# A fused block-sparse attention and MLP kernel: mask factors padded to 128 rows, w_in loads moved on POOL's queue, and new times in the planner

## The chip, the cores and the metric

The kernel runs on one core of a Trainium2 chip. The time is that of the device in microseconds for one execution; lower is better. Six runs of the kernel before gave a median of 275.79 us (274.7 to 276.76). One further execution was taken by the hardware profiler; every profile line below is from it.

## The reference

Attention under a block mask, and behind it a two-layer MLP with a gated activation, all in float32 at the interface:

```python
# q, k, v: [4 batches, 8 heads, 768, 64]; blocks of 32, so 24 x 24 blocks
mask = np.abs(blk_i - blk_j) <= 1
mask = mask | (blk_i == 0) | (blk_j == 0) | (blk_i == 23) | (blk_j == 23)
# and, for every block row, three sampled block columns: mask = True
scores = np.where(mask, q @ k.T / sqrt(64), -1e9)
x = softmax(scores) @ v              # -> [3072 tokens, 512]
h = x @ w_in                         # w_in: 512 x 2048
g = h / (1 + exp(-beta * h))         # beta: one for each of 2048 columns
out = g @ w_out                      # w_out: 2048 x 512
```

## The kernel before, in words

**Work and units.** Products are in float16 with float32 sums in PSUM. The 16 pairs of heads (4 batches times 4 pairs, numbered 0 to 15) and the query columns make units of 256 or 512 queries. A unit has score steps (`products`, L694), each of which fills two PSUM banks; one exponential of 128x1024 on ScalarE (`exps`, L698) empties them. For batches 1 to 3 VectorE then multiplies by a 0/1 mask (`masks`, L708). Value products follow (`av`, L731), VectorE divides by the row sums (`divide`, L740 and L742), and the quotient is turned by TensorE (`turn_pe`, L754) or by a DMA (`turn_dma`, L762). Seven groups of 256 or 512 tokens take the MLP: 16 hidden steps of four products with w_in (L787), a tanh on ScalarE (L794), a gate on VectorE (L800), then the products with w_out (L811), their eviction and the store. The silu is computed as half of (1 + tanh(beta h / 2)) h, and the half is applied at the eviction.

**Two kinds of mask.** Batch 0 carries the mask inside the score product: 24 extra rows of keys and queries, so that K and Q have 88 rows (64 + 24). Batches 1 to 3 have score products of 64 rows, and the 0/1 mask `mask01` (128 x 6 x 768) is built once, by 12 products of TensorE (L653), six of 512 columns and six of 256, with contraction over the 24 blocks (`NB` rows of both factors):

```python
nc.tensor.matmul(ps[:, 0:n], lhsT=seen.rearrange("i j r -> i (j r)")[:, c:S:NC],
                 rhs=oh_q[:, q0 // P:(q0 + n) // P, :], start=True, stop=True)
```

`oh_q` is copied by POOL (L885) from a one-hot table, `seen` is written by VectorE (`seen_step`, L647). Each product is evicted to `mask01` by VectorE (L512).

**Order.** TensorE's order is a string written out by hand (`order`, L956 on): S is a score step, V a value step, T a turn, H a hidden step, O or o a step of the output products, X an extra. The extras come from a list in fixed order (L938 to L954): turns of the keys and first queries of pairs 1 to 3, the turn of beta, turns of the late queries (columns 256 to 767) of pairs 0 to 3, mask products, turns of pair 4, mask products. Each has a time `at` before which the planner does not place it.

`weave` (L67) is a planner that runs when the program is built. It walks through the string with a model of the engines' clocks (costs such as .903 for an exponential, .432 for a score step of batch 0; start time `t0`; arrival times `W_IN`, `W_OUT` and the extras' `at`). It never alters TensorE's order. It decides two things: the order of the instructions on ScalarE and VectorE, and which PSUM bank each step takes. `Banks.one` (L48) takes the bank that is free first in the plan's time; among those that count as free it prefers the one whose partner in the pair came (or comes) free last:

```python
with_it = now + 20.0 if e[b ^ 1] is None else min(e[b ^ 1], now + 20.0)
able.append((max(e[b], now), -with_it, b))
```

`Banks.pair` (L42) does the same for the two banks of a score step. On the chip an instruction waits until the earlier readers of its bank have ended, whatever the plan thought.

**POOL's queue** (L860 to L890) is a list too, and its instructions run in that order: casts of keys, values and late queries to float16, and between them the issues of DMA loads. The four quarters of w_in (`load_w_in`, 512 KB each) are issued at L876, L878, L881 and L884; the one-hot copy and the loads of pair 4 and of w_out follow. Hidden step f reads quarter f // 4 of w_in. The loads that SP issues at the start (k, q, v of pairs 0 to 3) are L563 to L576.

Of the kernel before, what the change touches and what calls it, by code (L numbers as in the profile page):

```python
# [11 lines left out]
FP16 = mybir.dt.float16  # L12
AF = mybir.ActivationFunctionType
# [50 lines left out]
            self.ends[b] = t  # L64


def weave(order, units, moes, extras, beside, flush, t0=6.5):  # L67

    PE_OUT, ACT_OUT, DVE_OUT = .20, .16, .12
    W_IN = (21.0, 24.3, 27.7, 31.0)
    W_OUT = (37.0, 40.3, 43.7, 47.0)
    clock = {"PE": t0, "ACT": t0, "DVE": t0 + 1.0}
    queue = {"ACT": [], "DVE": []}
    banks = Banks()
# [28 lines left out]
    def one_bank(*after):  # L107

        if None in after:
            return None  # L110
        t = max(after)
        b = banks.one(max(t, clock["PE"]))
        return b and (max(t, b[0]), b[1])
# [149 lines left out]
    def hidden():  # L263
        g, f = hs[0]
        if groups_left[g]:
            return None
        b = one_bank(arrived[g], W_IN[f // 4] if g == 0 else 0.0, gb.free() if f == 0 else 0.0)
        return b and (b[0], lambda t: do_hidden(g, f, b[1], t))

    def do_hidden(g, f, b, t):  # L270
        hs.pop(0)
        m = moes[g]
        if f == 0:
            g_use[g] = gb.take()
        banks.take(b)
        m["h"](f, b)
        end = whole(t, 4 * (m["n"] / 2400.0 + .002))
        if f == 15:
            xt.end(xt_use[g], end)

        def tanh_done(e):
            kt = tsb.take()
            put("DVE", lambda: e + ACT_OUT, .07 + m["n"] * .00104, 1, lambda: m["gate"](f),
                lambda e2: gate_done(e2, kt))

        def gate_done(e, kt):
            tsb.end(kt, e + DVE_OUT)
            banks.end(e + DVE_OUT, b)
            gates[g] = gates.get(g, 0) + 1
            if gates[g] == 16:  # L290
                g_ready[g] = e + DVE_OUT
        put("ACT", lambda: None if tsb.free() is None else max(end, tsb.free()),
            .143 + .00083 * m["n"], 0, lambda: m["tanh"](f), tanh_done)

    def outs(rows=False):
        g, ts, part = os_[0]
        if g not in g_ready:
            return None
        after = max(g_ready[g], W_OUT[part] if g == 0 else 0.0)
        if part:  # L300
# [36 lines left out]
    while True:  # L337
# [3 lines left out]
        if state["next"] < len(order):  # L341
            c = kinds[order[state["next"]]]()
# [31 lines left out]
def kernel(  # L374
# [11 lines left out]
    nc = tc.nc  # L386

    B, H, S, D = q.shape
    BLK = 32
    NB = S // BLK  # L390
    P = 128
    NC = S // P
    NPAIR = H // 2
# [11 lines left out]
    persist = ctx.enter_context(tc.tile_pool(name="persist", bufs=1))  # L405
# [50 lines left out]
    def load(i, name, c0=0, c1=NC, split=False, eng=nc.sync, and_then=None):  # L456
        b, j = seq[i]
        x = {"k": k, "q": q, "v": v}[name]
        if (i, name) in first_in_w_out:
            at = 1024 + 2 * 2 * NC * D * first_in_w_out.index((i, name))  # L460
            loaded[(i, name)] = (w_out_sb.rearrange("p f m -> p (f m)")
                                 [:, at:at + 2 * 2 * NC * D].bitcast(FP32)
                                 .rearrange("p (h x) -> p h x", h=2))
        elif (i, name) not in loaded:
            loaded[(i, name)] = stage_pool.tile(
                [P, 2, NC * D], FP32, tag="sq" if name == "q" else "skv", name=f"{name}st")
        st = loaded[(i, name)]
        src = x[b, 2 * j:2 * j + 2].rearrange("h (p c) d -> p h (c d)", c=NC)
        for h in ((0, 1), (1, 2)) if split else ((0, 2),):
            eng.dma_start(out=st[:, h[0]:h[1], c0 * D:c1 * D],  # L470
                              in_=src[:, h[0]:h[1], c0 * D:c1 * D])
            if and_then is not None:
                and_then()
                and_then = None

    def cast(i, name, eng, c0=0, c1=NC, h0=0, h1=2):
        dst = (va_tiles[i % NVA] if name == "v" else
               (k_rows if name == "k" else q_rows)[i % NST] if i < NPAIR else
               packed(i)[name == "q"].rearrange("p c (h d) -> p h c d", h=2))
        st = loaded[(i, name)].rearrange("p h (c d) -> p h c d", d=D)  # L480
        eng.tensor_copy(out=dst[:, h0:h1, c0:c1, 0:D], in_=st[:, h0:h1, c0:c1, :])  # L481

    def packed(i):

        return [r[i % NST].rearrange("p h c s -> p (h c s)")[:, 0:NC * P]
                .rearrange("p (c s) -> p c s", s=P) for r in (k_rows, q_rows)]
# [39 lines left out]
    def turned_by_pe(i, which, h, c0, c1):  # L526

        rows = (k_rows, q_rows)[which][i % NST]

        def pe(b):  # L530
            tp = bank16(b)[:, 0:NC, :]
            for c in range(c0, c1):
                nc.tensor.transpose(out=tp[0:KR, c, :], in_=rows[:, h, c, 0:KR],  # L533
                                    identity=identity)
            return tp

        def copy(tp, on_act, a=c0, z=c1):
            evacuate(kq[i][which][0:KR, h, a * P:z * P],
                     tp[0:KR, a:z, :].rearrange("p c s -> p (c s)"), on_act)
        return pe, copy  # L540
# [11 lines left out]
    def load_w_in(i):  # L552
        nc.gpsimd.dma_start(out=w_in_sb[:, :, i * 512:(i + 1) * 512],
                            in_=w_in_r[:, :, i * 512:(i + 1) * 512])
# [23 lines left out]
    zeros = persist.tile([P, 256], FP16, name="zeros")  # L578
# [29 lines left out]
    oh_c = onehot.rearrange("i j r -> i (j r)").rearrange("i (p c) -> i c p", c=NC)  # L608
# [9 lines left out]
    for val in (0.0, float(NB - 1)):  # L618
# [3 lines left out]
            out=far, in0=iota_i[:, 0:1].to_broadcast([NB, NB]), scalar=val,  # L622
# [8 lines left out]
    mask16 = persist.tile([NB, NB], FP16, name="mask16")  # L631
# [8 lines left out]


    mask01 = persist.tile([P, NC, S], FP16, name="mask01")
    oh_q = persist.tile([NB, NC, P], FP16, name="oh_q")
    seen = persist.tile([NB, NB, BLK], FP16, name="seen")

    def seen_step():
        nc.vector.tensor_scalar(out=seen, in0=mask16.unsqueeze(2).to_broadcast([NB, NB, BLK]),  # L647
                                scalar1=0.0, scalar2=None, op0=ALU.is_equal)

    def mask01_task(c, q0, n):  # L650
# [12 lines left out]
    def beta_task():  # L663
        def pe(b):
            ps = psum[:, b, :]
            nc.tensor.transpose(out=ps[:, 0:N_FFC], in_=beta_sb, identity=ident[0:16, 0:16])
            return ps

        def copy(ps, on_act):
            nc.vector.tensor_scalar(out=beta_h_sb, in0=ps[:, 0:N_FFC], scalar1=0.5,  # L670
                                    scalar2=None, op0=ALU.mult)
        return pe, copy
# [169 lines left out]
    units = []  # L842
# [32 lines left out]
    cast(2, "v", nc.gpsimd)  # L875
    load_w_in(0)  # L876
    cast(3, "v", nc.gpsimd)
    load_w_in(1)  # L878
    for i in range(2):
        cast(i, "q", nc.gpsimd, 2, NC)  # L880
    load_w_in(2)  # L881
    for i in range(2, NPAIR):
        cast(i, "q", nc.gpsimd, 2, NC)
    load_w_in(3)  # L884
    nc.gpsimd.tensor_copy(out=oh_q, in_=oh_c)  # L885
    load(4, "k", eng=nc.gpsimd)
    load(4, "q", eng=nc.gpsimd)
    for i in range(4):
# [40 lines left out]
    extras = []  # L929

    def extra(first, need, at, took, task, eng, dur):
        box = {}
        extras.append(dict(
            first=first, need=need, at=at, took=took,
            pe=lambda b: box.update(ps=task[0](b)),
            out=(eng, dur, lambda: task[1](box["ps"], eng == "ACT"))))

    for i in range(1, NPAIR):  # L938
        at = (6.3, 9.2, 12.6)[i - 1]
        for h in range(2):  # L940
            extra(3 * i - 2, 3 * i, at, .34, turned_by_pe(i, 0, h, 0, NC), "DVE", .55)
        for h in range(2):
            extra(3 * i - 2, 3 * i, at, .12, turned_by_pe(i, 1, h, 0, 2), "DVE", .28)
    extra(8, 14, 9.0, .07, beta_task(), "DVE", .18)
    for i in range(NPAIR):
        for h in range(2):
            extra(6, 12 + 6 * i, (17.9, 18.5, 19.5, 21.3)[i], .23,
                  turned_by_pe(i, 1, h, 2, NC), "DVE", .42)
    for c in range(NC):
        extra(18, 36, 20.0, .22, mask01_task(c, 0, 512), "DVE", .6)  # L950
# [2 lines left out]
    for c in range(NC):  # L953
        extra(31, 60, 40.0, .11, mask01_task(c, 512, 256), "DVE", .35)  # L954
    cast(1, "q", nc.vector, 0, 2)
    order = (  # L956
        "SXXSXXSSXXXSXSVSXXSXSXVSXSXXXTSXXSSTVSSXSXVXSSSXVSVTSSTVSXHXHSSXHXHHSVSSVTSSSHXVHTSH"
        "HSHSXVTSHXHXVHSSHTHHHHSSHHHSSHHHHHHHSSXXVXSHSSVXHSoSoSSHVSSooSSVHSSXVVSoSSoSoSoSoSVV"
        "SSoSooSSVVOSSoSHHHHSSooSoSoSSoSoSVHVHHHVSSOHSSVHVSSHOSSVOSSSHOHVHHVHHSSHHHHSSOOSSSOH"
        "VSSHVSSHOHHHVSSooSSoSSoVHHHVVHHSSoooSoSoSoSoSSoooSSoSoSHHVSSHVHHHVHVSSooSoSoSoSoSSoS"  # L960
        "oSOVHHVHOVHVHHHHHSooSSooSSooSSooSoooSSoSooSHOVHOHHHHVHHTHHTVHHHHTVOHTOHHHHHHOHOOHOOH"
        "OHOHOHOHOOHOHHOOHOOOOOOOOOO"
    )
# [29 lines left out]
```

## Time and profile before

| | |
|---|---|
| median of six runs | 275.79 us |
| the profiled execution | 275.45 us |
| its span, first to last instruction | 273.7 us |
| TensorE busy | 266.3 us (97%) |
| VectorE busy | 204.6 us (75%) |
| ScalarE busy | 210.8 us (77%) |
| POOL busy | 61.0 us (22%) |
| chain that ended last | PE 86%, ACT 7%, DVE 2%, DMA 2%, issue 2% |

How to read what follows. PE is TensorE's products, PEld its weight loads, DVE VectorE, ACT ScalarE, POOL GpSimd, SP the engine that issues most DMAs. The chain follows the work back from the last instruction, at each step to what released it. L numbers are lines of the kernel before. A group such as "24*128 24x512 f16" is a product with weights of 24 rows and 128 columns and a moving operand of 24 rows and 512 columns; "88*128" and "64*128" are the score products of batch 0 and of the others. Brackets such as [1.32 <-ACT et L698] give the idle time ahead of an instruction and what ended it. Ends of TensorE's products are modelled, so records of neighbours overlap; the chain counts each stretch once. Between 13.6 and 19.7 us POOL issues the four loads of w_in with casts between them; they landed 6.7 to 9.2 us after their issue. Key and query columns reach TensorE first at 3.91 us, the exponentials begin at 7.49 us, the first hidden step is at 31.33 us and the first output product at 70.17 us.

### The profile page before, as it was taken

How to read it: one execution, taken by the hardware profiler on the slowest of the kernel's cores; microseconds unless marked ns; L12 is line 12 of the kernel's file. 1: busy time of each engine (PE TensorE's matmuls, PEld its weight loads, DVE VectorE, ACT ScalarE, POOL GpSimd, SP SyncE). 2: the span in 40 equal slices, each digit the busy share in tenths (PEclk: the TensorE clock that was granted, in tenths of full speed). 3: DMA queues.
4: the chain of work that ended last, by engine and by line, in shares of the span. 5: the costliest groups of instructions: out<-in, count | busy, mean ns of one | idle time of the engine just before them, and what ended most of it. 6: DMA issues, size and time to landing. Idle time of an engine off the chain costs nothing.

```text
span 273.7 us, 6832 instructions
## 1 busy us (share of the span) xinstructions
PE 266.3 (97%) x2774; PEld 150.4 (55%) x2774; DVE 204.6 (75%) x411; ACT 210.8 (77%) x276; POOL 61.0 (22%) x90
## 2 busy tenths in 40 slices
PE   8989999999999999999999999999999999999994
PEld 5876568544556645555345454464555555565541
DVE  6756657899999988899899786787867677863521
ACT  3879999898999799898898968979848866552300
POOL 4998508674022200330421000000000000000000
PEclk9999999999999999999999999999999999999999
DMA  6999998995499915375993131111120110011111
GB/s 199 367 245 214 250 263 294 244 273 180 86 245 230 187 51 185 95 194 109 230 248 89 29 79 42 58 42 25 73 41 38 41 77 2 0 41 40 51 65 77
DMA packets 46451, 36.23 MB, mean 132 GB/s; under 512 B 27844, under 2 KB 42388, under 8 KB 46420
## 3 DMA queue, kind: packets, MB, share of 16 engines
q1 hardware_dynamic: 40816, 26.89, 37.4%
q0 software_dynamic: 5568, 8.91, 14.8%
q8 instruction: 21, 0.34, 0.5%
q14 instruction: 10, 0.08, 0.1%
q10 hardware_dynamic: 36, 0.00, 0.0%
HBM read 27.27 MB, written 6.29 MB: 123 GB/s over the span
## 4 chain that ended last, share of the span: by engine, by line
PE 86%; ACT 7%; DVE 2%; issue 2%; DMA 2%; SPq 0%; POOL 0%; ACTq 0%
PE banks L811 29%; PE banks L787 27%; PE banks L731 13%; PE banks L694 13%; ACT et L698 5%; DMA kst<-in_k_dram 2%; ACT t_sb L794 2%; PE banks L533 1%; PE banks L653 1%; DVE et L708 1%; DVE g L800 1%; PE banks L754 1%; DVE xst L742 0%; SPq L470 0%; POOL kr L481 0%
## 5 line engine op out<-in xcount | busy, mean ns | idle before, releaser
L698 ACT ACTIVATE et<-banks 128x1024 f16<-128x1024 f32 x144 | 139.4, 1029 | 8.1 <-PE banks L694 7.2
L794 ACT ACTIVATE t_sb<-banks,beta_h_sb 128x512 f16<-128x512 f32 (+1 forms) x112 | 68.4, 634 | 36.4 <-PE banks L787 34.7
L787 PE MATMUL banks<-xt,w_in_sb 128*128 128x512 f16 (+1 forms) x448 | 93.5, 349 | 0.4 <-DVE g L800 0.4
L811 PE MATMUL banks<-w_out_sb,g 64*128 64x512 f16 (+1 forms) x612 | 93.7, 377 | 0.0
L708 DVE TENSOR_TENSOR et<-et,mask 128x1024 f16<-128x1024 f16 x108 | 77.4, 728 | 17.2 <-ACT et L698 15.6
L800 DVE SCALAR_TENSOR_TENSOR g<-t_sb,banks 128x512 f16<-128x512 f16 (+1 forms) x112 | 65.8, 605 | 20.4 <-ACT t_sb L794 20.0
L787 PEld LDWEIGHTS <-w_in_sb 128*128 128x128 f16 x448 | 40.8, 98 | 41.5 <-issue 6.7
L811 PEld LDWEIGHTS <-g 64*128 64x128 f16 (+1 forms) x612 | 37.0, 95 | 38.0 <-issue 1.3
L694 PE MATMUL banks<-qT,kT 64*128 64x256 f16 (+3 forms) x384 | 54.7, 325 | 0.3 <-DVE xst L742 0.2
L731 PEld LDWEIGHTS <-et 128*128 128x128 f16 x1152 | 40.9, 97 | 9.2 <-issue 2.7
L731 PE MATMUL banks<-va,et 128*128 128x65 f16 x1152 | 43.7, 193 | 0.1
L694 PEld LDWEIGHTS <-kT 64*128 64x128 f16 (+1 forms) x384 | 20.8, 95 | 19.4 <-issue 7.9
L481 POOL CAST kr<-kst 128x768 f16<-128x768 f32 (+1 forms) x15 | 13.3, 887 | 56.9 <-DMA kst<-in_k_dram 56.9
L742 DVE TENSOR_TENSOR xst<-banks,recip 128x256 f16<-128x256 f32 x48 | 20.4, 424 | 1.9 <-DVE recip L740 0.3
L481 POOL CAST va<-vst 128x768 f16<-128x768 f32 x13 | 12.3, 953 | 18.9 <-DMA vst<-in_v_dram 11.6
L740 DVE RECIPROCAL recip<-banks 128x4 f32<-128x4 f32 x48 | 8.5, 178 | 7.3 <-PE banks L731 7.0
L481 POOL CAST qr<-qst 128x768 f16<-128x768 f32 (+1 forms) x16 | 13.1, 830 | 2.3 <-DMA qst<-in_q_dram 2.0
L830 DVE SCALAR_TENSOR_TENSOR osb<-banks,osb 128x512 f32<-128x512 f32 x15 | 10.3, 685 | 1.5 <-ACT osb L824 1.4
L834 DVE TENSOR_SCALAR osb<-banks 128x512 f32<-128x512 f32 x9 | 6.2, 687 | 6.0 <-PE banks L811 6.0
L824 ACT ACTIVATE osb<-banks 128x512 f32<-128x512 f32 x15 | 9.1, 604 | 2.0 <-PE banks L811 2.0
L512 DVE CAST mask<-banks 128x512 f16<-128x512 f32 (+1 forms) x12 | 6.6, 554 | 3.2 <-PE banks L653 2.9
L512 DVE COPY qT<-banks 88x512 f16<-88x512 f16 (+2 forms) x16 | 5.4, 363 | 3.6 <-PE banks L533 3.2
(63 smaller groups left out, 78.7 us busy)
## 6 DMA issues: line engine op xcount, KB each, us to landing
out_dram<-osb SPq DMA_DIRECT2D x24, 256.0 KB, 2.0
kst<-in_k_dram SPq DMA_DIRECT2D x10, 384.0 KB, 3.7
vst<-in_v_dram SPq DMA_DIRECT2D x9, 384.0 KB, 4.9
qst<-in_q_dram SPq DMA_DIRECT2D x8, 384.0 KB, 4.0
w_in_sb<-in_moe_w_in_dram POOLq DMA_DIRECT2D x4, 512.0 KB, 8.1
w_out_sb<-in_moe_w_out_dram POOLq DMA_DIRECT2D x4, 512.0 KB, 13.6
kst<-in_k_dram POOLq DMA_DIRECT2D x4, 384.0 KB, 7.5
qst<-in_q_dram POOLq DMA_DIRECT2D x4, 384.0 KB, 8.4
```

The lines of the kernel that those rows point to most:

```text
L481: eng.tensor_copy(out=dst[:, h0:h1, c0:c1, 0:D], in_=st[:, h0:h1, c0:c1, :])
L512: nc.vector.tensor_copy(out=o, in_=i_)
L694: nc.tensor.matmul(sc[:, y, :], lhsT=lhsT, rhs=rhs, start=True, stop=True)
L698: nc.scalar.activation(out=et, in_=scs[x], func=AF.Exp, bias=0.0, scale=SCALE)
L708: nc.vector.tensor_tensor(out=et, in0=et, in1=m.unsqueeze(1).to_broadcast([P, 2, w, n]), op=ALU.mult)
L731: nc.tensor.matmul(at[:, z, qc, :], lhsT=ets[(hh, kc)][:, qc * P:(qc + 1) * P], rhs=va[:, hh, kc, 0:D + 1], start=(kc == 0), stop=(kc == N ...
L742: nc.vector.tensor_tensor(out=o, in0=at[:, :, :, 0:D], in1=recip.unsqueeze(3).to_broadcast([P, nh, nq, D]), op=ALU.mult)
L787: nc.tensor.matmul(hp[:, 0:n], lhsT=w_in_sb[:, c, f * P:(f + 1) * P], rhs=xt_tiles[group][:, c, 0:n], start=(c == 0), stop=(c == NPAIR - 1))
L794: nc.scalar.activation(out=t_sb[:, 0:n], in_=box[f][0][:, 0:n], func=AF.Tanh, bias=0.0, scale=beta_h_sb[:, f:f + 1])
L800: nc.vector.scalar_tensor_tensor(out=box["g"][:, f, 0:n], in0=t_sb[:, 0:n], scalar=1.0, in1=hp[:, 0:n], op0=ALU.add, op1=ALU.mult)
L811: nc.tensor.matmul(psum[:, b, :], lhsT=box["g"][r, f, ts * P:(ts + 1) * P], rhs=w_out_sb[r, f, :], start=z >= begun, stop=f == N_FFC - 1 o ...
L830: nc.vector.scalar_tensor_tensor(out=o_sb, in0=psum[:, bs[0], :], scalar=0.5, in1=o_sb, op0=ALU.mult, op1=ALU.add)
```

## The change

Three edits. First, `oh_q` and `seen` get 128 rows; two ScalarE copies of a zero tile clear them, and the one-hot copy and `seen_step` then write the first 24 rows as before. The mask products read the whole tiles, so they contract over 128 rows, 104 of them zero. Second, on POOL's queue the loads of w_in quarters 1, 2 and 3 stand behind the late-query casts of pairs 1, 2 and 3; before, quarter 1 stood ahead of these casts, quarter 2 behind the second cast and quarter 3 behind the fourth. Third, constants of the planner: `t0`, `W_IN`, `W_OUT`, and the `at` of the early turns, of beta and of the late-query turns. The order string and all costs in it stay.

```diff
--- before.py
+++ after.py
@@ -64,15 +64,15 @@
             self.ends[b] = t
-def weave(order, units, moes, extras, beside, flush, t0=6.5):
+def weave(order, units, moes, extras, beside, flush, t0=6.7):
     PE_OUT, ACT_OUT, DVE_OUT = .20, .16, .12
-    W_IN = (21.0, 24.3, 27.7, 31.0)
-    W_OUT = (37.0, 40.3, 43.7, 47.0)
+    W_IN = (22.0, 25.0, 27.5, 30.0)
+    W_OUT = (37.0, 39.5, 42.0, 44.5)
     clock = {"PE": t0, "ACT": t0, "DVE": t0 + 1.0}
     queue = {"ACT": [], "DVE": []}
     banks = Banks()
@@ -640,11 +640,15 @@
     mask01 = persist.tile([P, NC, S], FP16, name="mask01")
-    oh_q = persist.tile([NB, NC, P], FP16, name="oh_q")
-    seen = persist.tile([NB, NB, BLK], FP16, name="seen")
+
+    oh_q = persist.tile([P, NC, P], FP16, name="oh_q")
+    seen = persist.tile([P, NB, BLK], FP16, name="seen")
+    for x in (oh_q, seen.rearrange("p j r -> p (j r)").rearrange("p (c s) -> p c s", s=P)):
+        nc.scalar.activation(out=x, in_=zeros[:, 0:P].unsqueeze(1).to_broadcast([P, NC, P]),
+                             func=AF.Copy, bias=0.0, scale=1.0)
     def seen_step():
-        nc.vector.tensor_scalar(out=seen, in0=mask16.unsqueeze(2).to_broadcast([NB, NB, BLK]),
+        nc.vector.tensor_scalar(out=seen[0:NB], in0=mask16.unsqueeze(2).to_broadcast([NB, NB, BLK]),
                                 scalar1=0.0, scalar2=None, op0=ALU.is_equal)
     def mask01_task(c, q0, n):
@@ -875,14 +879,11 @@
     cast(2, "v", nc.gpsimd)
     load_w_in(0)
     cast(3, "v", nc.gpsimd)
-    load_w_in(1)
-    for i in range(2):
+    for i in range(NPAIR):
         cast(i, "q", nc.gpsimd, 2, NC)
-    load_w_in(2)
-    for i in range(2, NPAIR):
-        cast(i, "q", nc.gpsimd, 2, NC)
-    load_w_in(3)
-    nc.gpsimd.tensor_copy(out=oh_q, in_=oh_c)
+        if i:
+            load_w_in(i)
+    nc.gpsimd.tensor_copy(out=oh_q[0:NB], in_=oh_c)
     load(4, "k", eng=nc.gpsimd)
     load(4, "q", eng=nc.gpsimd)
     for i in range(4):
@@ -936,15 +937,15 @@
             out=(eng, dur, lambda: task[1](box["ps"], eng == "ACT"))))
     for i in range(1, NPAIR):
-        at = (6.3, 9.2, 12.6)[i - 1]
+        at = (8.0, 10.5, 12.8)[i - 1]
         for h in range(2):
             extra(3 * i - 2, 3 * i, at, .34, turned_by_pe(i, 0, h, 0, NC), "DVE", .55)
         for h in range(2):
             extra(3 * i - 2, 3 * i, at, .12, turned_by_pe(i, 1, h, 0, 2), "DVE", .28)
-    extra(8, 14, 9.0, .07, beta_task(), "DVE", .18)
+    extra(8, 14, 10.5, .07, beta_task(), "DVE", .18)
     for i in range(NPAIR):
         for h in range(2):
-            extra(6, 12 + 6 * i, (17.9, 18.5, 19.5, 21.3)[i], .23,
+            extra(6, 12 + 6 * i, (16.4, 17.0, 18.2, 19.5)[i], .23,
                   turned_by_pe(i, 1, h, 2, NC), "DVE", .42)
     for c in range(NC):
         extra(18, 36, 20.0, .22, mask01_task(c, 0, 512), "DVE", .6)
```

## The prediction

> **What bounds the kernel now.** I read the page's chain first (PE 86%, ACT 7%), then the chain in order of time around each place that the diff touches, then what PE, ACT and POOL waited for there. From 18.65 us to the end TensorE hardly ever has nothing to do, so the question is which of its time is not product time, and whether ScalarE lets a shorter TensorE be shorter. The chain at the first 0/1 mask products (L653; columns: start, length, piece):
>
> ```profile
> 26.36 0.35 PE banks L653
> 26.71 0.86 PE banks L731 x24
> 27.57 0.43 PE banks L694 x2
> 28.01 0.76 PE banks L731 x24
> ...
> 31.05 0.34 PE banks L653
> 31.39 0.54 PE banks L787 x4
> 31.94 0.35 PE banks L653
> 32.28 0.54 PE banks L787 x4
> ```
>
> One 512-column mask product takes 0.35 us of the chain; two 512-column score products take 0.43, so one such is worth 0.22. And what follows it is late as well: 24 value products take 0.86 after a mask product and 0.76 after the 88-row scores; four 256-column products take 0.54 instead of 0.44. The instruction forms say what differs (nanoseconds, least/median/most):
>
> ```profile
> L653 PEld LDWEIGHTS <-seen x12: 119/120/142, 26.3 to 79.3; 24*128 24x128 f16 x12
> L653 PE MATMUL banks<-oh_q,seen x12: 268/360/415, 26.3 to 79.3; 24*128 24x512 f16 x6, 24*128 24x256 f16 x6
> ```
>
> These are 24-row weights between 128-row and 88-row ones. The 88-row scores pass into 128-row work at no price (28.01), the 24-row ones pay going in and coming out. Second place, the only real stall of TensorE after the start, first from PE, then from ACT:
>
> ```profile
> 16.72 0.61 PE L694 MATMUL banks<-qT,kT 88*128 88x256 f16 x4
> 18.65 0.83 PE L533 MATMUL banks<-identity,qr 128*88 128x128 f16 x12 [1.32 <-ACT et L698]
> 19.32 0.27 PE L754 MATMUL banks<-identity,xst 128*128 128x128 f16 x2
> 19.43 0.60 PE L694 MATMUL banks<-qT,kT 88*128 88x256 f16 x4
> ```
>
> ```profile
> 15.71 2.88 ACT L698 ACTIVATE et<-banks 128x1024 f16<-128x1024 f32 x3
> 20.07 1.02 ACT L698 ACTIVATE et<-banks 128x1024 f16<-128x1024 f32 x1 [1.47 <-PE banks L694]
> ```
>
> The late-query transposes wait 1.32 us for the exponential that ends at 18.6, the last one queued; so ScalarE, until then the bound, empties and idles 1.47. Third, how much room ScalarE has (busy us of PE, PEld, DVE, ACT, POOL in each stretch):
>
> ```profile
> 19.00:31.00 12.00, 12.00 (x187) 8.47 (x184) 7.71 (x24) 10.89 (x12) 8.43 (x12) 1.00 1.17 231
> 31.00:50.00 19.00, 19.00 (x231) 12.85 (x230) 13.38 (x34) 17.44 (x27) 10.36 (x14) 1.00 1.11 261
> 50.00:62.00 12.00, 11.78 (x66) 5.38 (x65) 10.87 (x19) 12.00 (x19) 7.83 (x9) 1.00 1.10 266
> 62.00:80.00 18.00, 17.77 (x200) 8.88 (x200) 17.23 (x35) 17.14 (x23) 4.75 (x6) 1.00 0.56 170
> ```
>
> ScalarE has 1.56 us of idle time in 31 to 50, none in 50 to 62, 0.86 in 62 to 80. PE's clock column is 1.00 throughout.
>
> **Part 1, padding.** A mask product pays 0.13 on entry (0.35 less 0.22; for 256 columns 0.24 less 0.11), its follower 0.11. Seven (six of 512 columns and the first of 256, 26.3 to 48.1) stand between work of 88 or 128 rows: both charges go, 7 x 0.24 = 1.68. The other five stand among the 64-row scores: the pair at 64.59 and the one at 79.34 come from 64 rows, which still is a change, and save the exit (0.11 each); the one at 65.80 saves its entry (0.12); the one at 68.8 both (0.24). Sum 1.68 + 0.58 = 2.26 us of PE. The other end is nothing. The Trainium skill, "TensorE: Matmul & The Clock Gate", LDWEIGHTS: a weight load of 32 rows takes as long as one of 128, since columns set it. By that rule padding is worth 0; by the row the 24-row load takes 120 ns against 98 and[...] lies open. A second rule speaks against: "TensorEngine Tiling", Performance Considerations, wants up to 32 contraction rows as four row tiles side by side, which padding gives up. But in the trace the neighbouring pair takes 0.35 = 0.24 + 0.11, one after the other, and the others stand alone. I lose nothing and keep 2.26.
>
> Its price: two ACT copies, 128x768. ACT's 256-column rows take 0.47 to 0.49, the 1024-column ones 1.02, so by the line between some 0.84 each, 1.7 for both, and below 2.04. They are queued behind the warm-up (ends 2.90), need only the zeros of 0.87, and end by 4.6 (at most 4.94); behind them the key copy waits for PE until 4.81. Nothing, at most 0.13, and even that meets ACT's later idle 0.95 and 0.42 ahead of the first exponential. The DVE and POOL steps still write 24 rows: no change.
>
> **Part 2, w_in.** On POOL, a load's issue takes 0.74 (first 0.89), a late query cast 0.56 to 0.62. Casts 0, 1, 2 move up by 0.74 if their rows have landed; cast 3 keeps its place. Load 1 is issued at about 16.4 instead of 15.28, load 2 about 0.5 later, load 3 and the one-hot copy as before. Landing took 6.7 to 9.2 us, so load 1 is there by 25.6; its first reader is the fifth hidden step at 35.3. Cover 9.7 us. Behind it on POOL two loads of the next pairs wait for w_in (0.51 and 1.95), so they may go up to 0.6 later; POOL then waits 8.53 for a value load till 41.95, whose first product is at 64.94, and the pair-4 casts at 32 are first transposed at 45.0. No SP instruction is moved. I count 0; without the cover it would be those 1.1 us.
>
> **Part 3, the planner's times.** TensorE's order is a fixed string; the times only decide banks and the order on ACT and DVE. Worked through with the code's own costs (they only pick banks; no time is taken from them): with 17.9, the last exponential before the transposes is planned to free its pair at 17.78, so it counts as free, and `one` prefers the bank whose partner came free last, exactly that pair. The chip ends it at 18.61: the stall. With 16.4 the transposes come right behind the scores, planned at 17.3, when that exponential has not ended; the free banks are those of the first quotient, of beta and of an exponential two steps back. On the chip these are free by 17.0 and the casts done by 17.2. So the 12 transposes start near 17.35, the two of L754 and the scores follow (18.65 to 20.03 took 1.38), ending near 18.75: the next exponential starts about 18.75, not 20.07: gain 1.3. Against it: at 8.0 instead of 6.3 the first key transposes are planned after the first exponential, so the second score step takes that exponential's pair rather than a fresh one. It ends at 8.51, the scores started at 8.30: 0.25 late at once, and ScalarE runs almost unbroken from there. Net 1.05, bounds 0.7 to 1.4. The W_IN and W_OUT times lie before the planned start of what they gate (first hidden step about 30; L811 is 20 us behind W_OUT), so they move nothing.
>
> **Sum.** Part 3 moves PE and ACT together: 1.05. Of the 1.68 up to 50 us ScalarE must follow: it has 1.56 idle up to there, of which waits of the hidden steps keep some; I take 1.1. The ACT-bound stretch 50 to 62 starts that much earlier and keeps its length. Of the 0.58 later, ScalarE's 0.86 lets 0.45 through. That is 2.6. From 62 on the chain is PE up to 132, and ACT had just idled (0.93, waiting for PE) before its stretch there, so the shift carries to the end. Profiled execution: 275.45, of which span 273.7 and 1.75 around it. Span 271.1, execution 272.85; the median of the runs is 0.34 above the profiled one: **273.2**.
>
> **Rivals.** (a) ScalarE gives the padding back: 18.65 to 62 is ACT's work, so only part 3 and a few tenths come through, 1.3 in all: 274.5. For: ACT is 12.00 of 12 in 50 to 62. Against: its idle 1.05 at 48.7, just ahead, waited for PE. 0.15. (b) The padding doesn't do what it is for (the charge belongs to the changing tile, not to the rows): part 3 alone, 274.7. Against: the changes between 88-row and 128-row tiles are free. 0.05. (c) More than I count: all 2.26 plus 1.3, and smaller waits in 50 to 62 go with the nearer plan: 271.9. 0.12. (d) Slower: the new bank choice puts a stall like the one at 17.3 elsewhere. The plan runs ahead of the chip (first hidden step planned about 30, executed 31.33), so `one` can again hand out banks of exponentials not ended. Each costs up to ACT's 1.47 where ACT is the bound (7 to 19, 50 to 62, 132 to 142). The gain of 2.6 is used up by two such; with three the sum is 1.8 slower: 277.6. For: every bank after 8 us is chosen anew. Against: today's choice, no better informed, has one in 273 us. 0.10. The forecast has the remaining 0.58, with one or no small new wait, 272.2 to 274.4 by itself.
>
> A difference of 0.5% (1.4 us: 274.4 and 277.2) is about what a measurement of this kernel can tell. Faster: forecast 0.57, (c) 0.12, a little of (a) 0.04: 0.73. Slower 0.09. Same 0.18. The range 271.8 to 275.0 leaves out most of (d) and the best of (c).
>
> **What will show it.** L653 on 128 rows, 0.22 and 0.11 in the chain and 0.76 or 0.44 behind it: part 1. No PE wait at 17.3 and exponentials unbroken to 30: part 3; a second exponential at 9.2 instead of 8.94: its cost. Hidden steps never waiting for w_in: part 2. ACT's idle at 48.7 nearly gone: the room used. I am wrong if ACT idles as much before 50 while PE waits there, or if new PE waits for banks appear.

## The result, and the profile after

The changed kernel took 274.15 us (median of 37 runs, 272.26 to 276.35), the kernel before 276.10 in the same comparison. The ratio is 0.9928, with a 95% interval of 0.9913 to 0.9944: 2.0 us faster (1.5 to 2.4) where 2.6 was forecast. The profiled execution took 273.73, its span is 271.9 (before: 275.45 and 273.7).

First the chain at the first mask products (columns: start, length, piece). The line that builds them is now L657; L698 are scores, L735 values, L791 hidden products.

```profile
26.57 0.22 PE banks L657
26.79 0.75 PE banks L735 x24
27.54 0.43 PE banks L698 x2
27.98 0.76 PE banks L735 x24
...
31.02 0.22 PE banks L657
31.24 0.44 PE banks L791 x4
31.67 0.22 PE banks L657
31.89 0.44 PE banks L791 x4
```

A mask product of 0.35 us has become one of 0.22; the values behind it take 0.75 as against 0.86, the hidden products 0.44 as against 0.54. Both charges are gone, to the hundredth. Next comes TensorE where it had waited 1.32 us, and then ScalarE there:

```profile
18.40 0.61 PE L698 MATMUL banks<-qT,kT 88*128 88x256 f16 x4
18.85 0.83 PE L533 MATMUL banks<-identity,qr 128*88 128x128 f16 x12
...
19.63 0.60 PE L698 MATMUL banks<-qT,kT 88*128 88x256 f16 x4
```

```profile
10.34 1.02 ACT L702 ACTIVATE et<-banks 128x1024 f16<-128x1024 f32 x1 [1.76 <-PE banks L698]
11.54 11.61 ACT L702 ACTIVATE et<-banks 128x1024 f16<-128x1024 f32 x12 [0.18 <-PE banks L698]
```

There is no wait behind the scores now, and the exponentials run unbroken through 18.6 and past 20. But the second exponential starts at 10.34, not at 8.94 as in the profile of before: this execution lost 1.4 us in its start and so shows less than was won. A start as late is in the second profile of the kernel before too (below). Two of the stretches (busy us of PE, PEld, DVE, ACT, POOL, then clock, DMA share, GB/s):

```profile
31.00:50.00 19.00, 19.00 (x244) 14.15 (x242) 14.07 (x36) 18.23 (x29) 10.05 (x14) 1.00 1.18 263
...
62.00:80.00 18.00, 17.91 (x234) 9.81 (x233) 17.58 (x35) 17.77 (x22) 6.73 (x8) 1.00 0.75 218
```

ScalarE's idle time between 31 and 50 us has shrunk from 1.56 to 0.77: the room was used.

The order of the instructions on TensorE, ScalarE (but for the two copies of zeros) and VectorE is the same in both kernels. Worked through with its own rules, the planner's new times change the banks of TensorE's first 36 steps, up to about 21 us; behind those they only swap the names of the pairs (0, 1) and (2, 3), but for ten steps near the end.

**A measure that every run has.** VectorE takes 48 reciprocals, one for each value step, in one order in all kernels. Their times, less those of the first profile of before (in brackets), say where each execution stands: a minus is earlier. A kernel's own gain is read from one column to the next; the first column is its start.

| run | 1st (13.2) | 3rd (22.3) | 12th (49.4) | 22nd (95.3) | 23rd (108.8) | last (239.0) |
|---|---|---|---|---|---|---|
| before, again | +1.39 | +1.39 | +1.39 | +1.18 | +1.18 | +1.26 |
| w_in order alone | +0.31 | +0.31 | +0.31 | -0.16 | -0.15 | -0.18 |
| 64 rows alone | -0.43 | -0.43 | -0.42 | -1.03 | -1.02 | -1.00 |
| 128 rows alone | +0.77 | +0.76 | -0.67 | -0.73 | -0.72 | -0.96 |
| planner's times alone | +1.26 | -0.23 | -0.22 | +0.53 | +0.54 | +0.55 |
| late-query times alone | -0.25 | -1.40 | -1.33 | -1.22 | +0.24 | +0.23 |
| 128 rows, w_in, late-query times | +0.83 | -0.60 | -1.96 | -2.01 | -0.91 | -0.79 |
| the change | +1.69 | +0.20 | -1.22 | -1.60 | -1.60 | -1.72 |
| the change, again | +1.30 | -0.18 | -1.62 | -1.97 | -0.26 | -0.20 |
| change with zero products | -0.02 | -1.50 | -2.93 | -3.68 | -1.94 | -2.04 |
| change, pair 11 later | +1.26 | -0.22 | -1.66 | -1.13 | -1.13 | -0.97 |
| 128 rows, w_in, late-query times, pair 11 later | -0.06 | -1.50 | -2.85 | -1.78 | -1.78 | -1.88 |
| change with both | +0.67 | -0.82 | -2.25 | -1.11 | -1.11 | -1.25 |

### The profile page after: what moved, and what is told of

The parts are those of the page before. It is cut to its first block, busy times and chain, and to the rows that moved or that the text cites. A ratio compares the mean times of both kernels' runs of the same rounds, so it can differ in the third digit from the quotient of the medians.

```text
span 271.9 us, 6832 instructions
## 1 busy us (share of the span) xinstructions
PE 265.2 (98%) x2774; PEld 152.5 (56%) x2774; DVE 204.5 (75%) x411; ACT 211.7 (78%) x278; POOL 61.4 (23%) x90
## 4 chain that ended last, share of the span: by engine, by line
PE 87%; DVE 4%; ACT 3%; DMA 2%; issue 1%; SPq 0%; POOL 0%; ACTq 0%
PE banks L815 30%; PE banks L791 26%; PE banks L698 14%; PE banks L735 13%; DVE et L712 2%; DMA kst<-in_k_dram 2%; ACT et L702 2%; PE banks L533 2%; ACT t_sb L798 1%; PE banks L657 1%; PE banks L758 1%; DVE g L804 1%; DVE xst L746 0%; SPq L470 0%; DVE mask L512 0%
## 5 line engine op out<-in xcount | busy, mean ns | idle before, releaser
L815 PE MATMUL banks<-w_out_sb,g 64*128 64x512 f16 (+1 forms) x612 | 94.7, 377 | 0.1
L791 PE MATMUL banks<-xt,w_in_sb 128*128 128x512 f16 (+1 forms) x448 | 93.4, 349 | 0.4 <-DVE g L804 0.4
L791 PEld LDWEIGHTS <-w_in_sb 128*128 128x128 f16 x448 | 41.2, 98 | 41.1 <-issue 5.7
L815 PEld LDWEIGHTS <-g 64*128 64x128 f16 (+1 forms) x612 | 37.9, 95 | 38.5 <-issue 2.1
L698 PE MATMUL banks<-qT,kT 64*128 64x256 f16 (+3 forms) x384 | 56.8, 328 | 0.1
L735 PEld LDWEIGHTS <-et 128*128 128x128 f16 x1152 | 41.3, 97 | 8.6 <-issue 2.2
L735 PE MATMUL banks<-va,et 128*128 128x65 f16 x1152 | 43.6, 193 | 0.1
L698 PEld LDWEIGHTS <-kT 64*128 64x128 f16 (+1 forms) x384 | 22.0, 96 | 18.8 <-issue 7.7
L481 POOL CAST kr<-kst 128x768 f16<-128x768 f32 (+1 forms) x15 | 12.7, 849 | 55.1 <-DMA kst<-in_k_dram 55.1
L481 POOL CAST va<-vst 128x768 f16<-128x768 f32 x13 | 11.6, 898 | 18.9 <-DMA vst<-in_v_dram 10.8
L481 POOL CAST qr<-qst 128x768 f16<-128x768 f32 (+1 forms) x16 | 14.5, 908 | 2.8 <-DMA qst<-in_q_dram 2.8
```

The costliest lines, as they stand in the source:

```text
L698: nc.tensor.matmul(sc[:, y, :], lhsT=lhsT, rhs=rhs, start=True, stop=True)
L735: nc.tensor.matmul(at[:, z, qc, :], lhsT=ets[(hh, kc)][:, qc * P:(qc + 1) * P], rhs=va[:, hh, kc, 0:D + 1], start=(kc == 0), stop=(kc == N ...
L791: nc.tensor.matmul(hp[:, 0:n], lhsT=w_in_sb[:, c, f * P:(f + 1) * P], rhs=xt_tiles[group][:, c, 0:n], start=(c == 0), stop=(c == NPAIR - 1))
L815: nc.tensor.matmul(psum[:, b, :], lhsT=box["g"][r, f, ts * P:(ts + 1) * P], rhs=w_out_sb[r, f, :], start=z >= begun, stop=f == N_FFC - 1 o ...
```

## The experiments

**The padding alone.** As in the diff of the change, without its other two parts.

> The kernel before with the padding alone (two ScalarE copies of zeros, factors of 128 rows). Theory A (the prediction's): both tile changes go at seven mask products and one or two at the others; the mask products take 0.22 and 0.11 in the chain, TensorE is 1.5 to 1.7 us earlier at 50 us, 1.1 to 1.6 of it reach the end: 274.5 to 275.0 against 276.1, with the wait of 1.32 at 17.3 still there. Theory B (the planner's times alone are what helped, since ScalarE is full from 20 to 62): a gain of 0.3 or less.

The result is 0.9967 of before (0.9937 to 0.9997), 274.83 us. The wait of 1.32 is still there, the mask products take 0.22. In the table it wins 1.43 us between 22 and 49. So theory A holds and theory B falls, by the profile: the time alone (0.1 to 1.7 us won) would not exclude B's 0.3.

**The planner's times alone.** All constants of the change, 24-row factors, old order on POOL.

> The kernel before with the planner's times alone. Worked through with the planner's own rules, they change banks in the first 36 steps of TensorE only (to about 21 us), and behind that swap the names of two pairs, with no change of order on any engine. Theory A: the wait at 17.3 goes, ScalarE's idle 1.47 at 18.6 with it, the second exponential is 0.25 later: 1.05 faster (0.7 to 1.4). Theory B (the early choice costs what the late one gives: in the profile of the change the late query turns start at 18.85, 0.2 later than before): within 0.3 of before.

The result is 0.9967 (0.9938 to 0.9996), 275.42 us. The wait is gone: 1.49 us are won between the first and the third column. Then 0.75 is lost between 49 and 95, part of it in a wait of 0.9 us of the hidden products for a gate. The step is theory A's, and the whole lies inside A's bounds, but its interval reaches from 0.1 to 1.7 us.

**The late-query times alone.**

```diff
-            extra(6, 12 + 6 * i, (17.9, 18.5, 19.5, 21.3)[i], .23,
+            extra(6, 12 + 6 * i, (16.4, 17.0, 18.2, 19.5)[i], .23,
```

> The kernel before with only the four times of the late query turns changed (17.9, 18.5, 19.5, 21.3 to 16.4, 17.0, 18.2, 19.5). The first 26 steps keep their banks, so the second score step keeps a fresh pair. Theory A: the wait of 1.32 goes with no price at the start: 1.3 faster, 0.25 more than all planner times together, second exponential at 8.9. Theory C (the wait at 17.3 only absorbed time that ScalarE then makes up, since it has 1.56 us of idle between 31 and 50): 0.3 or less.

The result is 0.9989 (0.9966 to 1.0013), 275.77 us: not told from before. Yet 1.15 is won by 22 us. Theory C's number came, but not at its place: the lead is there at 49 and at 95 us (-1.33 and -1.22) and is lost at one point behind, where TensorE waits 1.33 us for a quotient that a DMA transposes.

**The change with the early times set back.**

```diff
-def weave(order, units, moes, extras, beside, flush, t0=6.7):
+def weave(order, units, moes, extras, beside, flush, t0=6.5):
...
-        at = (8.0, 10.5, 12.8)[i - 1]
+        at = (6.3, 9.2, 12.6)[i - 1]
...
-    extra(8, 14, 10.5, .07, beta_task(), "DVE", .18)
+    extra(8, 14, 9.0, .07, beta_task(), "DVE", .18)
```

(`W_IN` and `W_OUT` are set back too.)

> The change with the early planner times (6.3, 9.2, 12.6, beta, start, w_in, w_out) set back as before: padding, the order of the w_in loads and the late query times stay. Theory A: 0.25 faster than the change, which measured 0.9928 of before: 0.9919 or so, 273.9. If the early bank choice costs more, since TensorE then waits longer there and its clock falls (in the profile of the change it was 0.5 from 8 to 11 us), up to 1.4 faster than the change: 272.8. If it costs nothing, the same as the change.

The result is 0.9929 (0.9904 to 0.9954), 273.92 us: the same as the change, so the early bank choice has no price that a time shows. The wait for the transposed quotient is here as well, 0.97 us.

**The order of pair 11's transpositions on SP.** On the kernel of the last experiment:

```diff
-            if cast_at[i] + 2 == x and i > NPAIR:
+            if cast_at[i] + (4 if i == 11 else 2) == x and i > NPAIR:
```

> Padding, w_in order and late-query times as in the run of those three, and one DMA order changed: SP turns the keys and queries of pair 11 two score steps later, so that the last quotient transposition of the first 512-column hidden group stands ahead of them, not behind. In the run without it TensorE waited 0.97 us at 96.8 for that transposition, issued 4.6 us after its quotient was there. Theory D (what is won before 95 us is given back to SP's queue, whose DMA transposes run one behind another from 77 to 98 us): that wait goes, 0.7 to 1.0 faster than without, 0.989 to 0.990 of before. Theory E (that wait is chance, SP's order is of no account): 0.993, and the wait or another of its size stays.

(In the run that this text speaks of, the transposition was issued 4.1 us after its quotient was there, and landed 4.6 us after its issue.) The result is 0.9887 (0.9856 to 0.9918), 273.71 us. The wait is gone, as theory D has it. In time the run is not told from the kernel without the edit (0.9929, on another chip), since the intervals overlap; by the table this execution had also lost 1.07 between 49 and 95 us, 0.7 of it by 66, ahead of the edit's place.

**The order of the w_in loads alone.**

```diff
-    load_w_in(1)
-    for i in range(2):
+    for i in range(NPAIR):
         cast(i, "q", nc.gpsimd, 2, NC)
-    load_w_in(2)
-    for i in range(2, NPAIR):
-        cast(i, "q", nc.gpsimd, 2, NC)
-    load_w_in(3)
+        if i:
+            load_w_in(i)
```

> The kernel before with the new order of the w_in loads and late query casts on POOL alone. All theories: nothing (within 0.3), no wait of the hidden steps for w_in; the second load about 1.1 later, landing before 27, its first reader at 35. If it were not so, part of the change's gain or loss would be here.

The result is 1.0009 (0.9988 to 1.0031), 276.42 us: nothing. The loads land 5.7 to 9.8 us after their issue, and no hidden step waits for them.

**Factors of 64 rows.** As the padding, with 64 in place of 128 for `oh_q`, `seen` and the zeros.

> The kernel before with the factors of the mask products padded to 64 rows instead of 128. Theory A (the charge is for a change of the row class, 64 with 64 and 128 with 88 being alike): the seven products between 128-row and 88-row work keep 0.35 (0.24 for 256 columns) and the late followers, those next to 64-row scores lose the charge on that side: 0.11 at 65.8 between scores and 0.11 less behind. Theory F (the charge is for 24 rows as such, an odd count): 0.22 everywhere, as with 128 rows.

There is one execution only, 274.45 us, so the profile decides. Between 22 and 49 us it wins nothing, where 128 rows win 1.43. The chain follows, first among 88-row and 128-row work, then behind 64-row scores; L656 is the mask product, L697 the scores, L734 the values. The third piece is the same place in the kernel before:

```profile
25.93 0.35 PE banks L656
26.28 0.86 PE banks L734 x24
27.14 0.43 PE banks L697 x2
27.57 0.76 PE banks L734 x24
```

```profile
63.45 0.54 PE banks L697 x4
63.98 0.21 PE banks L656 x2
64.20 0.86 PE banks L734 x24
```

```profile
64.12 0.54 PE banks L694 x4
64.66 0.35 PE banks L653 x2
65.00 0.86 PE banks L731 x24
```

Among 88-row and 128-row work it is 0.35 and 0.86, as with 24 rows. Behind scores of 64 rows the two products take 0.21 (at 63.98) where those of 24 rows took 0.35: no entry charge there. So it is not 24 as such that costs, but the passage between three classes: 24 rows, 64 rows, and 88 together with 128. The weight loads tell what it isn't (first those of 64 rows, then those of the change; least/median/most in ns):

```profile
L656 PEld LDWEIGHTS <-seen x12: 121/122/124, 25.9 to 78.2; 64*128 64x128 f16 x12
```

```profile
L657 PEld LDWEIGHTS <-seen x12: 124/125/148, 26.2 to 78.0; 128*128 128x128 f16 x12
```

With 128 rows the load takes 125 ns, no less than the 120 ns with 24.

**Zero products at the start.** On the change:

```diff
+    keep_warm(2)
     turn_by_pe(0, 0, 1, 0, NC, 3, ((0, 3, True), (3, NC, False)))
...
+        if x == 0:
+            keep_warm(4)
         if x in (3, 6):
```

> The change with six more idle products of zeros in places where TensorE waits for the first keys (two ahead of the turn of the second head, four behind the first score step). In the profile of the change the clock column is 0.50 from 8 to 11 us and the second exponential starts at 10.34; before it was 1.00 and 8.94. Theory G (idle time of TensorE from 5.5 to 7.9 us lets the clock fall, and 0.8 to 1.7 of start is lost in most executions): first quotient near 13.3 instead of 14.9, 0.5 to 1.4 faster than the change. Theory H (the clock falls in few executions, and what is lost there is taken up later): the same as the change within 0.3.

The result is 0.9899 (0.9872 to 0.9925), 273.78 us; the first quotient is at 13.22, as theory G has it. Its profile then lost 1.74 us at the transposed quotient. In time it can't be told from the change, so neither G nor H is settled.

**The kernel before, profiled again.**

> The kernel before, unaltered, profiled once more: how far one execution's start differs from another's. Its wait of 1.32 at 17.3 and the mask products of 0.35 are the same in every execution; the first quotient (13.24 in the first profile) may be up to 1.7 later, and the span with it.

It took 276.72 us, span 274.9: 1.39 later at the first quotient, and still 1.26 later at the last. Here are the first products of TensorE in this execution, then those of the kernel with zero products (the last two lines of each are the twelve turns of the second pair's keys and the second score step):

```profile
6.85 1.06 PE L694 MATMUL banks<-qT,kT 88*128 88x256 f16 x4
7.70 1.49 PE L533 MATMUL banks<-identity,kr 128*88 128x128 f16 x12
8.98 1.06 PE L694 MATMUL banks<-qT,kT 88*128 88x256 f16 x4
```

```profile
6.57 0.60 PE L698 MATMUL banks<-qT,kT 88*128 88x256 f16 x4
...
7.45 0.83 PE L533 MATMUL banks<-identity,kr 128*88 128x128 f16 x12
8.29 0.60 PE L698 MATMUL banks<-qT,kT 88*128 88x256 f16 x4
```

They are the same products at little over half the pace; the clock column nevertheless says 1.00 for this execution from 6 to 11 us, while for the change's first profile it says 0.50 from 8 to 11. The twelve turns take 1.49 to 1.51 us in six of the fourteen profiles: this one, the change with the early times set back, and all four that have the new early times without zero products (the planner's times alone, the change twice, the change with pair 11 later). The new early times did not slow them: by the planner's own rules the second score step, behind these turns, is the first step whose bank they change.

**The change, profiled again.**

> The change, unaltered, profiled once more. The chain behind 20 us is that of its first profile; the first quotient (14.93 there) may be as early as 13.3, and then everything to 95 us is up to 1.7 earlier, unless TensorE then waits for the quotient transposition near 96 as in two other runs.

The result is 0.9924 (0.989 to 0.9958), 273.94 us. At 95 us this execution is 0.37 ahead of the change's first profile, at 109 us 1.34 behind. Here is TensorE at the first hidden step of the first 512-column group, and SP ahead of it:

```profile
95.10 0.82 PE L791 MATMUL banks<-xt,w_in_sb 128*128 128x512 f16 x3
97.50 2.97 PE L791 MATMUL banks<-xt,w_in_sb 128*128 128x512 f16 x13 [1.57 <-DMA xt<-xst]
```

```profile
88.08 0.52 SPq L842 DMA_DIRECT2D out_dram<-osb  x1
89.12 1.21 SPq L504 DMA_TRANSPOSE kT<-kr  x1
90.44 1.22 SPq L504 DMA_TRANSPOSE qT<-qr  x1
91.76 1.22 SPq L766 DMA_TRANSPOSE xt<-xst  x1
```

The fourth product needs the last pair's quotient. It was ready near 88.2; its transposition was issued at 91.76, behind an output store and the keys and queries of pair 11, and landed at 97.45. Those keys and queries belong to the last pair of the next batch.

**Pair 11 later, on the change.** The edit of x_spq.

> The change with the DMA order of pair 11 alone (its keys and queries turned behind the quotient transposition). Theory D: the room at 96 us lets all through that is won before, 0.3 to 0.8 faster than the change. Theory E: the same as the change.

```profile
89.63 1.68 SPq L766 DMA_TRANSPOSE xt<-xst  x1
91.42 1.23 SPq L504 DMA_TRANSPOSE kT<-kr  x1
```

```profile
95.94 3.66 PE L791 MATMUL banks<-xt,w_in_sb 128*128 128x512 f16 x16
```

The transposition is issued 2.1 us earlier and the sixteen products run through. The time doesn't settle it: the ratio is 0.9892 (0.9851 to 0.9933), but the median is 274.10 as against 273.94 of the change in the same comparison, and 0.53 is lost between 49 and 95 us in this profile, where the change won 0.35 to 0.38. All three profiles with the edit lost 0.5 to 1.1 there, of which 0.35 to 0.7 by 66 us. Beyond that, this profile loses 0.4 to the change's first one at 86 to 89 us, and this too comes before the first issue that the edit moves (89.63). Here is what POOL and VectorE did there, first in the change's first profile, then in this one:

```profile
86.76 0.69 DVE L712 TENSOR_TENSOR et<-et,mask 128x1024 f16<-128x1024 f16 x1
86.97 1.17 POOL L481 CAST qr<-qst 128x768 f16<-128x768 f32 x1 [0.23 <-DMA qst<-in_q_dram]
```

```profile
86.81 0.83 POOL L481 CAST qr<-qst 128x768 f16<-128x768 f32 x1
86.82 1.36 DVE L712 TENSOR_TENSOR et<-et,mask 128x1024 f16<-128x1024 f16 x1
```

The same multiplication by the mask takes 1.36 us when POOL's cast began just ahead of it and 0.69 when it began ahead of the cast. The quotients behind it come that much later, and TensorE goes on to the next scores 1.25 us after the start of the output products ahead of them instead of 0.86. The first profile of before, which has no edit, shows the same there (1.33, and 1.25).

**Both edits on the change.**

> The change with both, pair 11 behind the quotient transposition and six products of zeros at the start. If each gives what its own run gave (0.9887 and 0.9899 of before, against 0.9928 of the change) and they add, 0.986 to 0.988; if both only remove the same lateness, 0.989.

The result is 0.9882 (0.9842 to 0.9922), 273.73 us: the lowest ratio of all, but not told apart from the change (0.9924 beside it). The interval holds both what was expected if they add and what was expected if they don't. Here the first products kept their pace, yet the first quotient came only at 13.91, since TensorE waited 1.16 us for the cast of pair 2's keys.

## Why the prediction held, and where it didn't

**Padding (right; one reason wrong).** Entry 0.13 and exit 0.11 were the charges, and both went; 1.35 to 1.44 of 1.68 are won between 22 and 49 us in every profile with 128 rows, and nothing with fewer. I let 1.1 through, so I took ScalarE too seriously: it gave 0.79 of its idle time. Rivals (a) and (b) fall. The reason "the 24-row load takes 120 ns against 98" is wrong: the load takes 125 with 128 rows, and the charge went all the same. The rule that I set against the change ("TensorE: Matmul & The Clock Gate", LDWEIGHTS: rows don't count) is right about the load; it just isn't about what costs. That is in the Trainium skill's "TensorEngine Tiling (Array Packing)", Key Properties: changing the tiling mode drains TensorE, changing the tile within one mode doesn't. With its row tilings of 32, 64 and 128 rows (Available Configurations) the run with 64 rows agrees, and the traces give the price here: 0.13 in, 0.11 out. Behind 62 us I expected 0.45; the chain there shows a predicted form (one entry is left, 0.24 at 78.05 behind 64-row scores, and the values after it take 1.52 for 48, so no exit), but this execution passed 63.6 to 68.8 us through VectorE (17.58 of 18 us busy in the stretch), and no gain can be read from it.

**The copies (right).** They take 0.83 us each, the second from 3.53; the next copy still waited for TensorE until 4.72.

**w_in (right).** It gives nothing, measured alone.

**The planner's times (right; size off).** The wait went for the reason given. Won between the first quotient and the third: 1.43 to 1.49 in all kernels with the new late-query times but the one with those alone (1.15), where I had 1.3. The early price of 0.25 lies ahead of the first column, so I take it from the records: from the start of the second pair's key turns to the second score step it is 0.71 and 0.73 us with a fresh pair (late-query times alone, before) and 0.83 and 0.84 with the early choice (both kernels with zero products, which keep the pace); where the pace is half, 1.28 (before again) and 1.32 (the change again). So it is about 0.1, not 0.25. The ground of rival (d), that every bank after 8 us is chosen anew, was wrong: behind 21 us all but ten steps keep their bank under another name. No new wait for a bank shows in the profiles of the change.

**The carry to the end (wrong).** "From 62 on the chain is PE up to 132 [...] so the shift carries to the end" is the step that failed. By 95 us both profiles of the change had won 3.3 of their own start, more than the 2.6. (3.1, if the second profile of before is the measure; the first one had lost some time to the slow multiplication at 88 us.) Then the second profile lost 1.71 at one point, SP's queue. That queue runs almost without a gap from 78.2 to 98.7 us in the kernel before, and in all eleven profiles with SP's old order the transposition stands in it for 2.8 to 4.1 us after its quotient is ready.

From issue to use the transposition then has 3.8 to 4.5 us in the five with the old late-query times and 3.5 to 4.0 in the six with the new ones, so the change did not take the room away. What differs is the landing: 3.1 to 3.7 us after the issue in seven profiles, among them all five with the old times, and 4.6 to 5.7 in four, all with the new ones. These four waited 0.97 to 1.61 us. A landing as late would have been waited for in the kernel before too. With the queue rearranged the room is 7.0 to 7.6 us, and none of the three waited. Why the landing is late in some executions is not shown; nor is it shown that the new times make it more likely, since four of six against none of five is few. The transposition ahead of it in the queue took 4.8 to 5.4 us in every profile.

The 3.3, less 1.0 to 1.7 in the greater part of the executions, agrees with the 2.0 (1.5 to 2.4) measured; that this is the whole difference is not shown, since rearranging the queue took the wait away and no time that can be told apart. I had checked SP only for what the change moves ("No SP instruction is moved"), not for how little room it left. That the sum came so near is in part luck: more was won early than I counted, and some of it was lost at a place where I had not looked.

**50 to 95 us (a cause that I had not seen).** Near kernels differ here between 0.75 won and 1.14 lost. I had counted 50 to 62 us as ScalarE's stretch; the profiles point to VectorE's mask multiplications and POOL's casts. Over the fourteen profiles the 1194 multiplications of 128x1024 that meet no POOL work take 0.67 to 0.70 us, as do the 85 that began ahead of it; the 233 that begin while POOL is at work take 0.68 to 1.86. Added up over 49 to 95 us, the time above 0.69 is 1.5 to 4.3 us, and the profiles with more of it take longer for the stretch (correlation 0.92). From the 17th to the 22nd reciprocal (81 to 95 us) four profiles have an additional slow one, the first of before and the three with pair 11 later: they take 13.97 to 14.27 us, the other ten 13.56 to 13.72. In those three the slow one begins at 85.4 to 86.8 us, ahead of the first issue that their edit moves (88.7 to 89.6), so this loss is not the new order of SP's queue; that it fell on all three of them is not explained. No run here moves the casts away from the multiplications, so what that would be worth is not shown.

**Open.** What lets the transposition land late, and which execution loses the 0.7 to 1.7 us in its start.

## What to carry to other kernels

A short product whose rows fall in another class (24, 64, 88 to 128 here) than its neighbours' pays for its passage twice, 0.24 us in all, with 512 columns as with 256. Rows of zeros up to the neighbours' class took that away and cost nothing on TensorE (two copies of 0.83 us on an idle ScalarE); a class between did not help. Before a gain is carried to the end, ask of each transfer that has a deadline how long it stands in its queue and how much room is left from its issue to its use, against the spread of its landings; a transfer with an early deadline should not stand behind one with a late one. When profiles are compared stage by stage, take the start out first: here it differs by 1.4 us between two executions of the kernel before, and by 2.1 over all profiles, as much as the change is worth. And look for what two engines do to each other before a loss is put down to an edit.

## What was not expected of the hardware

The first products run at about half pace in some executions, of the kernel before as well (12 turns in 1.49 us as against 0.83 to 0.90), and the clock column shows it in one case (0.50) and not in another (1.00): durations of known products are the surer sign. In the two profiles with six zero products in the gaps they ran at full pace, but so they did in three of the profiles without, so that the zeros did it is not shown. The same DMA transposition landed after 3.1 to 3.7 us in seven executions and after 4.6 to 5.7 in four. A multiplication on VectorE took up to 1.86 us instead of 0.69 when a cast on POOL was under way as it began; when it began first it kept its 0.69, and the cast took longer (1.17 instead of 0.83 in the lines above).
